# All transfers of the first batch ahead of the first weights, and products of a zero tile behind the first ten steps of a fused retention and mixer kernel

## The chip, the cores and the metric

The kernel runs on one core of a Trainium2 chip. The metric is the device time of one execution in microseconds (us), and less is better. The core has five engines that run side by side and wait for one another by semaphores: TensorE (PE in the rows; PEld is its weight load), VectorE (DVE), ScalarE (ACT), GpSimd (POOL) and SyncE (SP). SP issues every transfer of this kernel. The clock of TensorE has two levels, 1.2 and 2.4 GHz, and the rows show the granted share as PEclk, 0.50 or 1.00.

## What is computed

Three stages follow each other on 8 batches of 576 positions, 8 heads of 64 channels (512 channels in all):

```python
scores = q @ k.T / 8;  ret = scores * gamma[h] ** (i - j) for i >= j, else 0
x = ret @ v                                   # retention, heads side by side
u = x + (x.T @ U @ V).T                       # mix over positions, rank 32
x2 = u + relu(u @ w_ch1) @ w_ch2              # 512 -> 2048 -> 512
xk, xr = mu * x2 + (1 - mu) * x2_prev         # each position with the one before
out = sigmoid(xr @ w_r) * (relu(xk @ w_k) ** 2 @ w_v)
```

U, V and the weights arrive as float64 words and are turned into float32 on the chip.

## The kernel before

**Steps.** Retention is done in chunks of 64 positions: nine steps for each batch, 72 in all, listed in `seq` and run by `step_of(i)`. A step issues four groups of sixteen 64x64 products each: `scores(i+1)` (L792) for the next step, `inter(i)` (L817, the queries with the state), and `own(i)` (L833 the new state, L845 the chunk itself). VectorE then does `decay(i+1)` (L804) and, in `leave(i)`, three operations: y (L866), the state w (L878) and the output xt (L884). Tile `up` holds the scores and the inter products, `dn` the own products; each has one buffer. Every second step a finished block of 128 positions is transposed (`natural`, L892), copied by ScalarE as xs (L902), and some steps later multiplied with U (`low_rank`, L913). GpSimd scales each piece of k by a table (`scale_k`, L763).

**After a batch.** Step 10 starts with `low_rank_sum(0)`: ScalarE copies the sum (gs, L928) and casts it (gt, L932 and L935), and VectorE makes a remainder (L934). Eight products with V follow (`mix`, L943), VectorE adds them to xt (L947), `split_u` makes two parts of the result, and from then on `hidden(1)` issues twelve dense 128x512 products (L336) in each step: the product of u with w_ch1. These are the hidden products.

**Weights.** A weight piece (128x512 words, 512 KB) takes four stages, made by `convert`: load (a transfer to w_raw), down (ScalarE, L104, to `ca`, which has two buffers), fill (three VectorE operations, L110, L114 and L119) and split (ScalarE casts the first part, L127, and GpSimd subtracts to get the second, L128). `place(get, down, fill, split)` hangs the stages of the next weight piece in the list `waiting` on numbers of steps in `early`, and `stages(i)` issues those of step i behind the step's own work; numbers below zero stand for places ahead of step 0. So for the first four pieces (0, 4), (0, 5), (2, 6), (2, 8) say: loaded at step 0, 0, 2, 2 and filled at step 4, 5, 6, 8. U and V go the same way.

**Order.** The whole is under a manual schedule: each engine runs its instructions in the order of the code. SP's queue is one of these; its transfers use eight semaphores in turn, so a transfer is issued when the one eight places earlier has landed. `load_to(i)` issues the loads of q with k (qk) and k with v (kv), two chunks to a piece, that are due by step i. Twelve products of a zero tile (`warm`, L1039, 128x512) stand ahead of step 0.

Of the kernel before, what the change touches and what calls it, by code (L numbers as in the profile page):

```python
# [30 lines left out]
NL = S // L  # L31
KD = DM // 128
WARM = 12
# [6 lines left out]
def retention_mixer_kernel(ctx: ExitStack, tc: tile.TileContext, io):  # L40
    nc = tc.nc
# [22 lines left out]
    def bank(n, nm):  # L64
        return psum[-1].tile([128, 512], F32, tag=f"b{n}", name=nm, bufs=1)

    turns = {}


    def turn(kind, banks, nm):  # L70
        i = turns.get(kind, 0)
        turns[kind] = i + 1
        return bank(banks[i % len(banks)], nm)
# [58 lines left out]
    waiting, going = [], []  # L132
# [13 lines left out]
    class Weight:  # L146
# [45 lines left out]
        def load(self, pool, j):  # L192
            for lo, parts in enumerate((self.h, self.l)):
                parts[j] = unit(pool, F32R, f"{self.nm}u{j}{lo}")
                nc.sync.dma_start(parts[j].bitcast(F32), self.kept[:, 2 * j:2 * j + 2, lo])
# [536 lines left out]
    with ExitStack() as st:  # L732
# [27 lines left out]
        def scale_k(b, p):  # L760
            n = 2 if p < NC - 1 else 1
            k = kv[b, p][:, :n, :256].rearrange("p c (h d) -> p c h d", d=D)
            nc.gpsimd.tensor_tensor(k, k, ktab[:, p, :n].to_broadcast([128, n, NP, D]), op=ALU.mult)  # L763
# [271 lines left out]
        warm = ac.tile([128, 1, 128], BF16, name="warm")  # L1035
        nc.vector.memset(warm, 0.0)
        nc.scalar.copy(omu[:, 0, 0:1], warm[:, 0, 0:1])
        for i in range(WARM):
            nc.tensor.matmul(  # L1039
                turn("u", ("n", "g"), f"warm{i}"),  # L1040
                warm[:, 0, :],
                warm.to_broadcast([128, 4, 128]),
                start=True,
                stop=True,
            )


        early = {}

        def place(*steps):  # L1050
            for i, stage in zip(steps, [x for x in waiting.pop(0) if x]):
                early.setdefault(i, []).append(stage)

        def stages(i):
            for stage in early.pop(i, []):
                stage()

        prep_u()
        place(-3, 0, 1, 2)
        place(-3, 1, 2, 3)  # L1060
        prep_v()
        place(-2, 2, 3, 4, 5)
        for w in w1:
            w.convert(big, big)
        for n, (get, fill) in enumerate((
            (0, 4), (0, 5), (2, 6), (2, 8), (5, 9), (6, 10), (7, 11), (8, 12),
            (9, 13), (9, 13), (10, 14), (11, 15), (12, 16), (12, 16), (13, 17), (14, 18),
        )):
            place(get, fill - 1, fill, fill + 1)

        for w in wv:
# [8 lines left out]
        def load_to(i):  # L1080
            while units and units[0][0] <= i:
                load(*units.pop(0)[1:])
# [1 line left out]
        load_to(0)  # L1084
        nc.sync.dma_start(dtab, io["dtab"])
        nc.sync.dma_start(ktab, io["ktab"])
        stages(-3)
        load_to(2)
        nc.sync.dma_start(qtab[:, 0], io["qtab"])
        nc.sync.dma_start(step, io["step"])  # L1090
        stages(-2)
        nc.sync.dma_start(ident, io["ident"])
        scale_k(0, 0)
        scores(0)
        decay(0)
        load_to(5)

        def next_qtab(p):
            for a in range(NP):
# [8 lines left out]
        def plan(i, fn, *args, where=due):  # L1108
            where.setdefault(i, []).append((fn, args))

        def step_of(i):
            b, c = seq[i]
            load_to(i + (5 if i < 4 or i > 11 else 4))
            for fn, args in first.pop(i, []):
                fn(*args)
            if i + 1 < N:
                nb, ncx = seq[i + 1]
                if ncx % 2 == 0:
                    scale_k(nb, ncx // 2)
                scores(i + 1)  # L1120
            inter(i)
            if i + 1 < N:
                decay(i + 1)
            own(i)
            leave(i)
            if c % 2 == 1 or c == NL - 1:
                last = c == NL - 1
                wait = 4 if i < 6 else 2 if last or b < 2 else 3
                plan(i + 1, natural, b, c // 2)
                where = first if last and b == 0 else due  # L1130
                plan(i + wait, low_rank, b, c // 2, where=where)
                if last and b == 0:
                    plan(i + wait, low_rank_sum, b, where=first)
                    plan(i + wait, later, b)
                elif last:
                    plan(i + wait, low_rank_sum, b)
                    plan(i + wait + 1, later, b)
            if i < 2 * NC - 2 and i % 2 == 0:
                next_qtab(i // 2 + 1)
            for fn, args in due.pop(i, []):  # L1140
                fn(*args)
            if not ready:
                mixes(9)
            few = i < 2 * NL + 2 or c == 7 or c == 4 and b > 3
            hidden(1 if few else 2, False)
            stages(i)
            if b > 1 and i > 2 * NL + 3 and not todo:
                quiet.append(i)
                slot(new=len(quiet) % 2 == 1)

        for i in range(N):
            step_of(i)
# [216 lines left out]
    for q in range(NB // 2 + 1):  # L1369
# [5 lines left out]
        if not last:  # L1375
            gates(q, (mine, other), 1 if q else 2)
            PUMP[0] = 2
            for g in range(NG):
                n = q * NG + g
# [101 lines left out]
```

## Time and profile before

| what | value |
|---|---|
| three runs | 1369.38, 1372.71, 1373.61 us |
| their median | 1372.71 us |
| profiled execution: span from the first to the last instruction | 1371.8 us (no other time is listed for it) |
| TensorE busy in the span | 1345.0 us, 98% |
| VectorE, ScalarE, GpSimd busy | 922.3, 625.0, 367.0 us |
| moved by transfers | 307.63 MB, mean 224 GB/s |

Shares of busy time are means over stages of very different kinds. TensorE's pipelined products count as busy while they are under way, at either clock, so a busy TensorE can still run at half its pace; PEclk tells which. In a row of the timeline, the number in brackets is how long the engine sat idle before, and the arrow names what ended that.

### The profile page before, as it was taken

Reading aid. Unit: us, or ns where it says so; the run is one execution under the profiler, and the core shown is the slowest. Engines: PE = TensorE matmul, PEld = TensorE weight load, DVE = VectorE, ACT = ScalarE, POOL = GpSimd, SP = SyncE. Lnnn points to the kernel's source line nnn. Section 1 sums busy time; section 2 is a strip of 40 time slices with the busy share of each in tenths; the row PEclk is TensorE's granted clock in tenths of the full one; section 3 lists DMA queues with packets and bytes.
Section 4 is the critical chain, followed back from the end, with each engine's and each line's share of the span. In section 5 each row is a group of like instructions: output and inputs, shape, how many; then the busy total and the mean of one; then the engine's idle time right before and its main releaser. Section 6 shows DMA issues by size and latency. Waiting matters only on the chain.

```text
span 1371.8 us, 26093 instructions
## 1 busy us (share of the span) xinstructions
PE 1345.0 (98%) x10296; PEld 1098.9 (80%) x10296; DVE 922.3 (67%) x1347; ACT 625.0 (46%) x1089; POOL 367.0 (27%) x301
## 2 busy tenths in 40 slices
PE   6899999999999999999999999999999999999998
PEld 4677777777877878887888888888888888888897
DVE  5873445342334156999798898687787787787753
ACT  4443334343333445554444544565455465465431
POOL 3250232322221245222211232203303303304212
PEclk8799999999999999999999999999999999999999
DMA  9667586967746475969888796797085075174272
GB/s 343 234 219 235 184 295 230 304 210 277 242 163 213 165 238 209 344 207 315 274 278 279 239 323 222 245 309 270 0 291 200 25 282 184 41 275 145 100 281 80
DMA packets 122762, 307.63 MB, mean 224 GB/s; under 512 B 15120, under 2 KB 27792, under 8 KB 122640
## 3 DMA queue, kind: packets, MB, share of 16 engines
q1 hardware_dynamic: 122640, 305.96, 64.5%
q8 instruction: 81, 1.33, 0.4%
q14 instruction: 41, 0.34, 0.1%
HBM read 214.69 MB, written 91.23 MB: 223 GB/s over the span
## 4 chain that ended last, share of the span: by engine, by line
PE 62%; DVE 2%; issue 0%; DVEq 0%
PE v L1326 14%; PE gc L521 6%; PE ga L521 6%; PE gd L521 6%; PE h L336 5%; PE kd L1230 4%; PE kc L1230 4%; PE ka L1230 4%; PE gb L521 3%; PE kb L1230 2%; PE rd L1230 2%; PE rc L1230 2%; PE ra L1230 2%; PE c L602 1%; PE c L601 1%; PE c L603 1%
## 5 line engine op out<-in xcount | busy, mean ns | idle before, releaser
L342 ACT ACTIVATE hs<-h 128x512 f32<-128x512 f32 x144 | 85.8, 598 | 249.3 <-PE h L336 241.4
L804 DVE TENSOR_TENSOR pm<-up,dtab 128x256 f32<-128x256 f32 x72 | 30.4, 422 | 164.0 <-PE up L817 148.2
L1282 POOL TENSOR_TENSOR vl<-m,vh 128x512 fp32r<-128x512 f32 (+1 forms) x40 | 47.7, 1194 | 310.1 <-ACT vh L1281 238.8
L480 ACT CAST sbh<-rb 128x1024 fp32r<-128x1024 f32 x64 | 67.4, 1053 | 54.0 <-PE gd L521 41.2
L1326 PE MATMUL v<-vh,wv_0u 128*128 128x512 f32 x288 | 88.7, 389 | 0.0
L1326 PE MATMUL v<-vh,wv_1u 128*128 128x512 f32 x288 | 88.6, 389 | 0.0
L481 DVE TENSOR_TENSOR sbl<-rb,sbh 128x1024 fp32r<-128x1024 f32 x64 | 85.3, 1333 | 1.9 <-ACT sbh L480 1.7
L481 DVE TENSOR_TENSOR sal<-ra,sah 128x1024 fp32r<-128x1024 f32 (+1 forms) x64 | 65.4, 1022 | 18.8 <-PE gd L521 10.9
L480 ACT CAST sah<-ra 128x1024 fp32r<-128x1024 f32 (+1 forms) x64 | 53.6, 837 | 53.7 <-DVE ra L462 21.1
L1282 POOL TENSOR_TENSOR vl<-c,vh 128x512 fp32r<-128x512 f32 (+1 forms) x40 | 62.2, 1575 | 25.9 <-ACT vh L1281 25.9
L1326 PEld LDWEIGHTS v<-vh,wv_1u 128*128 128x128 f32 x288 | 54.1, 188 | 11.2
L1326 PEld LDWEIGHTS v<-vh,wv_0u 128*128 128x128 f32 x288 | 53.9, 188 | 11.1
L947 DVE TENSOR_TENSOR xt<-mx,xt 128x256 f32<-128x256 f32 x64 | 28.8, 458 | 50.1 <-PE mx L943 50.1
L1281 ACT CAST vh<-m 128x512 fp32r<-128x512 f32 (+1 forms) x40 | 23.2, 579 | 75.3 <-DVE m L1280 75.3
L1326 PE MATMUL v<-vl,wv_0u 128*128 128x512 f32 x144 | 56.0, 389 | 0.0
L1326 PE MATMUL v<-vl,wv_1u 128*128 128x512 f32 x144 | 56.0, 389 | 0.0
L565 POOL TENSOR_TENSOR x<-x,ur 128x512 f32<-128x512 f32 x16 | 24.5, 1546 | 107.7 <-DVE x L561 51.2
L634 ACT ACTIVATE tp<-x2l,omu 128x511 f32<-128x511 f32 x72 | 50.9, 713 | 2.5 <-DMA x2l<-xb 2.5
L763 POOL TENSOR_TENSOR kv<-kv,ktab 128x512 f32<-128x512 f32 (+1 forms) x40 | 40.5, 1017 | 42.7 <-DMA kv<-in_kv 36.3
L792 PEld LDWEIGHTS up<-qk 64*64 64x64 f32 x1152 | 24.4, 137 | 31.8 <-issue 28.2
L538 POOL TENSOR_TENSOR m<-m,ur 128x512 f32<-128x512 f32 x8 | 12.3, 1554 | 126.3 <-ACT m L535 126.3
L1280 DVE SCALAR_TENSOR_TENSOR m<-m 128x512 f32<-128x512 f32 (+1 forms) x40 | 44.8, 1120 | 1.4
(289 smaller groups left out, 3876.4 us busy)
## 6 DMA issues: line engine op xcount, KB each, us to landing
wk<-keys SPq DMA_DIRECT2D x80, 512.0 KB, 6.0
hp<-hs SPq DMA_DIRECT2D x128, 256.0 KB, 3.4
rb<-hp SPq DMA_DIRECT2D x64, 512.0 KB, 6.1
wr<-gates SPq DMA_DIRECT2D x40, 512.0 KB, 7.1
qk<-in_qk SPq DMA_DIRECT2D x32, 512.0 KB, 5.0
kv<-in_kv SPq DMA_DIRECT2D x32, 512.0 KB, 5.6
ra<-hp SPq DMA_DIRECT2D x32, 512.0 KB, 6.9
ur<-ub SPq DMA_DIRECT2D x18, 512.0 KB, 5.9
```

What stands on the lines that cost most here:

```text
L336: nc.tensor.matmul(hps[t, f], w.part(lo, k, fo), u[k // 2][:, k % 2, :], start=(part == 0 and k == 0), stop=(part == 2 and k == KD - 1),)
L342: nc.scalar.activation(h, hps.pop((t, f)), AF.Relu)
L480: nc.scalar.copy(hi_, src)
L481: nc.vector.tensor_tensor(lo_, src, hi_.bitcast(F32), op=ALU.subtract)
L521: nc.tensor.matmul(group[g][p], l[:, col(p)], r, start=(h == 0 and j == 0 and i == 0), stop=(i == 2 and last), skip_group_check=True,)
L634: nc.scalar.activation(tp[:, 1:], x[:, :BT - 1], AF.Copy, scale=omu[:, j, k:k + 1])
L763: nc.gpsimd.tensor_tensor(k, k, ktab[:, p, :n].to_broadcast([128, n, NP, D]), op=ALU.mult)
L804: nc.vector.tensor_tensor(m, t[:, :, 0:128].rearrange("p g (a i) -> p g a i", i=L), dtab, op=ALU.mult)
L1230: nc.tensor.matmul(ps[b], l, r[:, i], start=(part == 0 and i == 0 and j == 0), stop=(i == 1 and j == 2), skip_group_check=True,)
L1280: nc.vector.scalar_tensor_tensor(x, x, 0.0, x, op0=ALU.max, op1=ALU.mult)
L1282: eng.tensor_tensor(l, x, h.bitcast(F32), op=ALU.subtract)
L1326: nc.tensor.matmul(vacc[t][o], w.part(lo, g, col(o)), x[:, i, :], start=(g == 0 and i == 0 and j == 0), stop=(g == NG - 1 and i == 1 and j ...
```

## The change

`idle(n, banks)` issues n products of the zero tile into the named banks of PSUM. It takes the place of the loop ahead of step 0, stands with three products behind the stages of each of the steps 0 to 9, and with four ahead of the scores that step 10 issues. The loads of all of batch 0's q, k and v are moved ahead of those of the first weights (`load_to(5)`, `load_to(6)`, `load_to(8)` ahead of step 0), and U and V behind some of them. U and V are converted two steps later. The first four weight pieces are all loaded at step 0 and filled at steps 7, 8, 8 and 8; the table of the later pieces is as it was.

```diff
@@ -1035,15 +1035,17 @@
         warm = ac.tile([128, 1, 128], BF16, name="warm")
         nc.vector.memset(warm, 0.0)
         nc.scalar.copy(omu[:, 0, 0:1], warm[:, 0, 0:1])
-        for i in range(WARM):
-            nc.tensor.matmul(
-                turn("u", ("n", "g"), f"warm{i}"),
-                warm[:, 0, :],
-                warm.to_broadcast([128, 4, 128]),
-                start=True,
-                stop=True,
-            )
-
+        def idle(n, banks):
+            for _ in range(n):
+                nc.tensor.matmul(
+                    turn("u", banks, f"warm{turns.get('u', 0)}"),
+                    warm[:, 0, :],
+                    warm.to_broadcast([128, 4, 128]),
+                    start=True,
+                    stop=True,
+                )
+
+        idle(WARM, ("n", "g"))
 
         early = {}
 
@@ -1056,16 +1058,23 @@
                 stage()
 
         prep_u()
-        place(-3, 0, 1, 2)
-        place(-3, 1, 2, 3)
+        place(-3, 2, 3, 3)
+        place(-3, 3, 4, 4)
         prep_v()
-        place(-2, 2, 3, 4, 5)
+        place(-2, 4, 5, 6, 7)
         for w in w1:
             w.convert(big, big)
-        for n, (get, fill) in enumerate((
-            (0, 4), (0, 5), (2, 6), (2, 8), (5, 9), (6, 10), (7, 11), (8, 12),
+        lead = [[x for x in waiting.pop(0) if x] for _ in range(4)]
+        for n, stage, i in (
+            (0, 0, 0), (1, 0, 0), (2, 0, 0), (3, 0, 0),
+            (0, 1, 6), (0, 2, 7), (1, 1, 7), (0, 3, 8), (1, 2, 8), (2, 1, 8), (1, 3, 8),
+            (2, 2, 8), (3, 1, 8), (2, 3, 8), (3, 2, 8), (3, 3, 9),
+        ):
+            early.setdefault(i, []).append(lead[n][stage])
+        for get, fill in (
+            (5, 9), (6, 10), (7, 11), (8, 12),
             (9, 13), (9, 13), (10, 14), (11, 15), (12, 16), (12, 16), (13, 17), (14, 18),
-        )):
+        ):
             place(get, fill - 1, fill, fill + 1)
 
         for w in wv:
@@ -1084,16 +1093,18 @@
         load_to(0)
         nc.sync.dma_start(dtab, io["dtab"])
         nc.sync.dma_start(ktab, io["ktab"])
-        stages(-3)
         load_to(2)
         nc.sync.dma_start(qtab[:, 0], io["qtab"])
         nc.sync.dma_start(step, io["step"])
-        stages(-2)
+        load_to(5)
         nc.sync.dma_start(ident, io["ident"])
+        stages(-3)
         scale_k(0, 0)
         scores(0)
         decay(0)
-        load_to(5)
+        load_to(6)
+        stages(-2)
+        load_to(8)
 
         def next_qtab(p):
             for a in range(NP):
@@ -1113,6 +1124,8 @@
             load_to(i + (5 if i < 4 or i > 11 else 4))
             for fn, args in first.pop(i, []):
                 fn(*args)
+            if i == NL + 1:
+                idle(4, (0, 1))
             if i + 1 < N:
                 nb, ncx = seq[i + 1]
                 if ncx % 2 == 0:
@@ -1144,6 +1157,8 @@
             few = i < 2 * NL + 2 or c == 7 or c == 4 and b > 3
             hidden(1 if few else 2, False)
             stages(i)
+            if i <= NL:
+                idle(3, (0, 1))
             if b > 1 and i > 2 * NL + 3 and not todo:
                 quiet.append(i)
                 slot(new=len(quiet) % 2 == 1)
```

On SP's queue, from batch 0's piece 2 on (qk_0 and kv_0 behind w_0 are batch 1's), before:

```order
L754 DMA qk_2_187<-in_qk 128x1024
L756 DMA kv_2_189<-in_kv 128x1024
L160 DMA w_0_raw_229<-in_moe_w_ch 128x512
L160 DMA w_0_raw_231<-in_moe_w_ch 128x512
L754 DMA qk_3_233<-in_qk 128x1024
L756 DMA kv_3_235<-in_kv 128x1024
L160 DMA w_0_raw_343<-in_moe_w_ch 128x512
L160 DMA w_0_raw_345<-in_moe_w_ch 128x512
L754 DMA qk_4_347<-in_qk 128x512
L756 DMA kv_4_349<-in_kv 128x512
L754 DMA qk_0_461<-in_qk 128x1024
L756 DMA kv_0_463<-in_kv 128x1024
```

and now:

```order
L754 DMA qk_3_186<-in_qk 128x1024
L756 DMA kv_3_188<-in_kv 128x1024
L1011 DMA vraw<-in_moe_V 32x144 x4
L754 DMA qk_4_195<-in_qk 128x512
L756 DMA kv_4_197<-in_kv 128x512
L160 DMA w_0_raw_235<-in_moe_w_ch 128x512
L160 DMA w_0_raw_237<-in_moe_w_ch 128x512
L160 DMA w_0_raw_239<-in_moe_w_ch 128x512
L160 DMA w_0_raw_241<-in_moe_w_ch 128x512
L754 DMA qk_0_475<-in_qk 128x1024
L756 DMA kv_0_477<-in_kv 128x1024
```

The pieces 3 and 4 of batch 0 stood behind two and four weight pieces; now all four weight pieces stand behind them. Piece 2 has moved up too, ahead of U and V (`uraw`, `vraw`).

On VectorE, at the end of batch 0 (names with numbers: pm8, y7, xt0 are step 8's decay and step 7's results in batch 0; w1_0_raw2 is the third of the first four weight pieces), before:

```order
L119 SCALAR_TENSOR_TENSOR cf_590<-w1_0_raw2_343,cf_590 128x512
L804 TENSOR_TENSOR pm8_618<-up8_601,dtab_114 128x256
L866 TENSOR_TENSOR y7_637<-up8_601,qtab_115 128x256
L878 TENSOR_TENSOR w0_7_639<-dn7_620,w0_6_572 128x256
L884 TENSOR_TENSOR xt0_219<-dn7_620,y7_637 128x4x64
L804 TENSOR_TENSOR pm9_670<-up9_653,dtab_114 128x256
L866 TENSOR_TENSOR y8_681<-up9_653,qtab_115 128x256
L884 TENSOR_TENSOR xt0_219<-dn8_672,y8_681 128x4x64
L110 TENSOR_SCALAR cf_691<-ca_648 128x512
L114 SCALAR_TENSOR_TENSOR cf_691<-ca_648,cf_691 128x512
L119 SCALAR_TENSOR_TENSOR cf_691<-w1_0_raw3_345,cf_691 128x512
```

and now:

```order
L866 TENSOR_TENSOR y8_709<-up9_681,qtab_115 128x256
L884 TENSOR_TENSOR xt0_227<-dn8_700,y8_709 128x4x64
L110 TENSOR_SCALAR cf_721<-ca_670 128x512
L114 SCALAR_TENSOR_TENSOR cf_721<-ca_670,cf_721 128x512
L119 SCALAR_TENSOR_TENSOR cf_721<-w1_0_raw1_237,cf_721 128x512
L110 TENSOR_SCALAR cf_731<-ca_725 128x512
L114 SCALAR_TENSOR_TENSOR cf_731<-ca_725,cf_731 128x512
L119 SCALAR_TENSOR_TENSOR cf_731<-w1_0_raw2_239,cf_731 128x512
L110 TENSOR_SCALAR cf_739<-ca_735 128x512
L114 SCALAR_TENSOR_TENSOR cf_739<-ca_735,cf_739 128x512
L119 SCALAR_TENSOR_TENSOR cf_739<-w1_0_raw3_241,cf_739 128x512
```

A fill used to have the operations of a step on either side; now three fills stand in a row behind step 8's xt0, ahead of the decay of step 10.

On TensorE, from step 1's own products to step 2's first group (up3 are the scores of step 3), before:

```order
L833 MATMUL dn1_257<-kv0_0_156 64x64 x8
L845 MATMUL dn1_257<-pm1_200,kv0_0_156 64x64 x8
L792 MATMUL up3_285<-qk0_1_163 64x64 x8
L817 MATMUL up3_285<-qk0_1_163,w0_1_276 64x64 x8
L833 MATMUL dn2_304<-kv0_1_165 64x64 x8
```

and now:

```order
L833 MATMUL dn1_269<-kv0_0_156 64x64 x8
L845 MATMUL dn1_269<-pm1_208,kv0_0_156 64x64 x8
L1040 LDWEIGHTS warm_123
L1040 MATMUL warm15_291<-warm_123 128x512
L1040 MATMUL warm16_293<-warm_123 128x512
L1040 MATMUL warm17_295<-warm_123 128x512
L792 MATMUL up3_297<-qk0_1_160 64x64 x8
L817 MATMUL up3_297<-qk0_1_160,w0_1_288 64x64 x8
```

The products of the zero tile stand between a step's own products and the next step's scores; the weight load stands ahead of each of the three.

## Rows read from the trace of the kernel before

**Rows 1.** The page: the span; one group (busy us, mean ns of one).

```profile
span 1371.8 us, 26093 instructions
...
L804 DVE TENSOR_TENSOR pm<-up,dtab 128x256 f32<-128x256 f32 x72 | 30.4, 422 | 164.0 <-PE up L817 148.2
```

**Rows 2.** Windows: length; busy us (count) by engine; PEclk, DMA share, GB/s.

```profile
0.00:10.00 10.00, 7.55 (x140) 3.98 (x140) 1.34 (x4) 2.12 (x4) 1.46 (x6) 1.00 0.85 281
...
10.00:20.00 10.00, 5.19 (x205) 4.25 (x200) 7.23 (x25) 5.44 (x18) 1.88 (x2) 1.00 0.94 310
...
20.00:29.00 9.00, 5.54 (x152) 4.58 (x156) 6.56 (x16) 6.08 (x18) 4.63 (x6) 0.80 1.03 409
...
29.00:39.00 10.00, 8.63 (x191) 6.53 (x184) 8.99 (x17) 3.90 (x8) 4.56 (x4) 0.50 1.03 407
...
39.00:42.40 3.40, 1.99 (x73) 1.37 (x72) 0.00 (x0) 3.15 (x8) 2.04 (x2) 1.00 0.24 95
...
42.40:47.90 5.50, 3.23 (x9) 2.20 (x9) 5.36 (x14) 1.87 (x4) 0.23 (x1) 0.50 0.00 0
...
47.90:52.60 4.70, 4.70 (x11) 3.41 (x12) 4.29 (x7) 1.31 (x3) 0.00 (x0) 0.50 0.74 250
...
52.70:95.00 42.30, 42.30 (x785) 33.10 (x785) 35.69 (x66) 23.50 (x46) 22.71 (x18) 1.00 0.79 275
...
95.00:1371.80 1276.80, 1265.73 (x8751) 1039.34 (x8749) 852.80 (x1202) 577.61 (x985) 329.51 (x265) 1.00 0.64 220
```

**Rows 3.** TensorE's timeline, 14 to 58 us: start, us, engine, line, operation, count.

```profile
14.48 0.46 PE L792 MATMUL up<-qk 64*64 64x64 f32 x16 [1.20 <-DMA qk<-in_qk]
...
16.14 0.46 PE L792 MATMUL up<-qk 64*64 64x64 f32 x16 [0.50 <-DVE y L866]
...
21.23 0.70 PE L792 MATMUL up<-qk 64*64 64x64 f32 x15 [3.04 <-DVE cf L110]
...
28.68 0.67 PE L792 MATMUL up<-qk 64*64 64x64 f32 x16
...
30.56 0.65 PE L913 MATMUL gall<-xs,ust 128*32 128x128 f32 x8
...
47.88 2.21 PE L336 MATMUL h<-uh,w_0h 128*128 128x512 f32 x4 [0.68 <-DVE xt L947]
...
53.11 0.46 PE L792 MATMUL up<-qk 64*64 64x64 f32 x16
...
54.20 0.66 PE L892 MATMUL xn<-ident,xt 128*128 128x128 f32 x4
...
54.61 1.18 PE L336 MATMUL h<-uh,w_0h 128*128 128x512 f32 x4
...
57.54 0.46 PE L792 MATMUL up<-qk 64*64 64x64 f32 x16
```

**Rows 4.** The chain that ended last, one piece: start, us, what, count.

```profile
487.37 73.75 PE h L336 x324
```

**Rows 5.** The timeline of all engines around one fill.

```profile
28.89 0.42 DVE L110 TENSOR_SCALAR cf<-ca 128x512 uint32<-128x512 uint32 x1
...
29.27 0.62 ACT L127 CAST w_0h<-cf 128x512 fp32r<-128x512 f32 x1
...
29.34 0.69 DVE L114 SCALAR_TENSOR_TENSOR cf<-ca,cf 128x512 uint32<-128x512 uint32 x1
...
29.97 1.27 POOL L128 TENSOR_TENSOR w_0l<-cf,w_0h 128x512 fp32r<-128x512 f32 x1 [2.64 <-ACT w_0h L127]
...
30.06 1.72 DVE L119 SCALAR_TENSOR_TENSOR cf<-w_raw,cf 128x512 uint32<-128x512 uint32 x1
```

**Rows 6.** The timeline ahead of the mixing.

```profile
40.19 0.69 ACT L104 ACTIVATE ca<-w_raw 128x512 f32<-128x512 f32 x1
...
40.78 1.05 ACT L928 COPY gs<-gall 32x128 f32<-32x128 f32 x4
...
42.51 0.68 DVE L934 TENSOR_TENSOR gt<-gs,gt 32x512 fp32r<-32x512 f32 x1 [3.52 <-ACT gt L932]
```

## Prediction

> **What bounds the kernel now.** I read the span on the page first [rows 1], then a table of stages [rows 2]: what matters there is TensorE's busy share, the granted clock and the transfer rate. From 95 us to the end TensorE is busy 1265.73 of 1276.80 us, and from 52.7 to 95 us all of the time, at the full clock. So the end follows the moment at which the dense hidden products begin; what is gained ahead of it comes off the total, unless it is given back later. That moment is the row at 47.88 in TensorE's timeline [rows 3]. Ahead of it lies a head in which TensorE works in small pieces: 5.19 of 10 us busy from 10 to 20, 5.54 of 9 from 20 to 29, and then 8.63 of 10 at half clock from 29 to 39. Two waits stand out: 1.20 us for a piece of batch 0's qk (14.48) and 3.04 us ahead of the row at 21.23, a step that reads the next piece (the profile names a conversion on VectorE there, which these products don't read). The transfers run at 409 and 407 GB/s in 20 to 39, their ceiling here, but only at 310 GB/s in 10 to 20, where the small rows of U and V fill places in SP's queue. The head ends on a chain: ScalarE copies the low-rank sum (40.78), VectorE waits 3.52 us for it (42.51) [rows 6], the mixing products follow, and the first hidden product comes 5.37 us after 42.51, at half clock: its twelve products take 53.11 - 47.88 = 5.23 us, the next twelve 57.54 - 54.61 = 2.93 [rows 3].
>
> **The change, part by part.**
>
> *Transfers.* Batch 0's q, k and v are 2 x 4.5 x 0.524 = 4.72 MB by their shapes; the tables, U and V with them make 5.49 MB. The first 10 us move 2.81 MB [rows 2]; the rest at 409 GB/s takes 6.6 us, so all has been moved at 16.6 us. Landing comes later. Now, the piece awaited at 21.23 has 5.50 MB issued up to it, and these had been moved at 18.7 us (2.81 MB, then 310 GB/s): at most 2.5 us of lag. So batch 0 is there between 16.6 and 19.1 us, and its last piece is first used in step 7, after 22. The wait of 1.20 goes, and that of 3.04. The first weights (four of 0.524 MB) land by 21.7 to 24.2, batch 1's first qk by 23.0 to 25.5. What is late next is the small identity table: it now stands behind two pieces of 0.524 MB, and the transpose of step 2 needs it at about 12.
>
> *Pace of the steps.* At full clock the four groups of a step's small products take 54.20 - 53.11 = 1.09 us and a transpose 0.41 more; at half clock the four groups take 30.56 - 28.68 = 1.88 [rows 3]. Three added products cost 3 x 73.75/324 = 0.68 us at full clock [rows 4]. They stand behind a step's own products and ahead of the next scores, where TensorE would wait for VectorE's y (0.50 us at 16.14); so 0.18 to 0.68 us a step shows, and I charge all of it. Step 3's scores without their wait start at 14.48 - 1.20 = 13.3. The added products of steps 0 to 2 and the identity push this to at most 13.3 + 3 x 0.68 = 15.3; I take 13.9, since TensorE is half idle there [rows 2]. Step 3 then takes 1.77, and steps 4 to 7, each with a transpose or a low-rank product (charged as a transpose), 2.18. Step 7 begins at 13.9 + 1.77 + 3 x 2.18 = 22.2, and its VectorE work, behind 1.09 us of products, is over about 0.8 us later, at 24.1.
>
> *Conversion of the first weights.* All four pieces are now filled at steps 7 (one) and 8 (three). A fill is 0.42 + 0.69 + 0.69 = 1.80 us of VectorE [rows 5], and there is a new neighbour. A filled piece is cast by ScalarE (0.62), and then GpSimd subtracts (1.27), while VectorE is in the next fill. The group [rows 5] shows what happens then: GpSimd starts at 29.97, and the VectorE operation of 30.06 takes 1.72 us instead of 0.69, until 0.54 us past GpSimd's end. Before, only one fill of the first weights met this, because the others had steps between them. The Trainium skill (SBUF — State Buffer, Who interferes with whom) makes it a lock that the first of the two holds for a whole instruction, so that up to 1.27 us are lost at each meeting; the row has 1.03. By the rule the three would cost 0.7 us more, and 1369.5 would come out of the sum below.
> Fill 0 ends at 24.1 + 1.8 = 25.9. Step 8's three VectorE operations (0.42 each [rows 1], less what they overlap, 1.0 in all) give 26.9. Three fills with a meeting each, 3 x 2.83 = 8.5, end at 35.4; without one, 3 x 1.80, at 32.3. This is the dear part of the change: the same 7.2 us were spread over steps 4 to 8 before, partly in VectorE's idle time.
>
> *From the last fill to the hidden products.* Two queues run in parallel. ScalarE casts (0.62), prepares another weight (0.69), copies the sum (1.05) and casts it (0.6, from 40.78 + 1.05 to 42.51): 38.4. VectorE does step 10's decay (0.4) and a fill with its meeting (2.83): 38.6. The later one starts what stood at 42.51, so that this comes 3.9 us earlier, and the hidden products at 44.0 instead of 47.88. The four products ahead of step 11's scores (0.91 us at full, 1.75 at half clock) lie in the wait for the low-rank sum and cost nothing; uncovered they would cost at most 1.75.
>
> *The clock at that point.* TensorE again has nothing to do between step 9's last product, near 30, and the low-rank product, near 35. Between 42.4 and 47.9 it was busy 3.23 of 5.50 us and the clock stayed at 0.50 [rows 2]; the same mixing products stand there now. I take the first twelve hidden products at half clock as before. Zero difference, with 2.3 us (5.23 - 2.93) to win.
>
> *Given back later?* All transfers up to the last ones ahead of the mixing land before 42.4 (95 GB/s in 39 to 42.4, none after [rows 2]); the 1.0 MB that 10 to 20 us fall short of 409 GB/s return 2.4 us, so that they land before 40 and still ahead of 44. Weights to come are filled in the same order against the hidden products, and TensorE waits for none of them in 52.7 to 95. I charge nothing; the bound is VectorE's slack there, 42.30 - 35.69 = 6.6 us.
>
> The sum: 1371.8 - 3.9 = 1367.9 for the span. The median of the three runs shown, 1372.71, is 0.9 above this span, so 1368.8.
>
> **The rivals.**
> - *As summed*, 1368.8, between 1367.2 (the steps hide 0.3 us of the added products each) and 1370.2 (step 3 at 15.3).
> - *The clock holds.* If the added products have it at full when the hidden ones begin, 2.3 us more are won: 1366.5. For it: the four products, the scores and step 10's work form some 4 us without a pause just ahead of the mixing. Against it: 42.4 to 47.9 [rows 2], where the mixing did not raise the clock. The Trainium skill (TensorE: Matmul & The Clock Gate, HAM oscillation) says that an engine left idle begins its next burst at half rate, and the added products work against that; the head agrees, and no run here shows the products doing it.
> - *VectorE and GpSimd don't meet.* Fills end at 32.3. ScalarE then decides: behind the third cast, over at 31.1, stand a preparation (0.69), three copies of step 9 (1.3, two casts' worth by size), and then the four operations (3.0), to 36.1. That is 6.4 us earlier than 42.51: 1366.3. Against it: the casts follow each fill at once, so GpSimd starts inside the next one, as at 29.97.
> - *The head hardly moves.* Step 3 only at 15.3, and 0.3 us more in each of steps 3 to 7, since VectorE's y and xt come late as at 16.14: 2.9 us of the gain go, 1371.7.
> - *Slower: the clock falls early and the added products become the pace.* At half clock a step takes 1.88 + 3 x 0.44 (5.23/12) = 3.19 instead of 1.77, with 0.41 more for its transpose. From step 3 on, 5 x 1.42 + 4 x 0.41 = 8.7 us are lost, 4.8 more than is won: 1377.5. It decides only if the clock is down by step 4, at about 16 us; in steps 6 and 7 alone it costs 3.7 and eats up the gain. Against it: 10 to 20 us kept the full clock with TensorE half idle [rows 2].
>
> **How the numbers follow.** Chances: as summed 0.45, the clock holds 0.20, no meeting 0.14, hardly moves 0.15, slower 0.06. About 0.3%, 4.1 us, is what a measurement of this kernel can tell from no change. The sum's 3.9 lies on that bound, so its chance is split, 0.19 faster and 0.26 within; with the next two, faster gets 0.53, within 0.42 (with the fourth and a little of the last), slower 0.05. The range goes from clock and meeting both being favourable, 1364, to a little above the head that hardly moves, 1372.2; 1364.5 leaves out the corner.
>
> **What would show it.** Right: no wait for qk or kv behind step 2; the last piece used at about 24; step 8's three fills as a block of some 8.5 us on VectorE with single operations of 1.6 to 1.8 us; TensorE idle some 4 to 5 us ahead of the low-rank product; the first hidden product near 44. Wrong: a granted clock of 0.50 between 10 and 25 us; fills of 1.8 us throughout; a first twelve that take 3 us; TensorE waits for weights between 50 and 95 us.

## The result, and the profile after

| what | before | after |
|---|---|---|
| median, us | 1373.16 (1369.38 to 1374.30, 4 runs) | 1380.99 (1378.40 to 1382.34, 4 runs) |
| span of the profiled execution, us | 1371.8 | 1378.2 |
| first hidden product (L336), us | 47.88 | 55.40 |
| scores behind the first twelve, us | 53.11 | 60.09 |

The ratio is 1.0058 with a 95% interval of 1.0043 to 1.0074: the change made the kernel slower, where 1368.8 us and a gain were forecast. The median lies 8.8 us above the upper end of the range. Line numbers of after: the products of the zero tile are L1040, the other lines of the head are as before.

The windows of after answer to [rows 2]; the last shows that the dense part hasn't changed (the one before it still holds some of the late head):

```profile
10.00:20.00 10.00, 7.23 (x226) 4.82 (x215) 6.47 (x21) 4.64 (x15) 3.04 (x4) 1.00 0.99 330
20.00:29.00 9.00, 5.16 (x146) 3.54 (x147) 3.61 (x12) 1.99 (x6) 0.60 (x1) 0.96 0.98 363
29.00:39.00 10.00, 7.92 (x189) 5.11 (x192) 6.29 (x15) 5.88 (x15) 2.54 (x6) 0.86 1.03 412
...
42.40:47.90 5.50, 2.17 (x12) 0.63 (x12) 5.36 (x8) 3.84 (x10) 2.94 (x3) 0.77 0.00 1
...
52.70:95.00 42.30, 41.62 (x644) 32.06 (x645) 38.76 (x71) 21.14 (x39) 18.26 (x14) 0.93 0.78 266
95.00:1378.20 1283.20, 1272.73 (x8907) 1044.97 (x8905) 857.73 (x1211) 582.71 (x995) 333.99 (x268) 1.00 0.63 220
```

In 95 us to the end TensorE is idle 10.5 us, and was idle 11.1 before. So the 6.4 us of the span were lost in the head. There, from 20 to 29 us, TensorE is busy 5.16 and VectorE 3.61 of 9.00 us (5.54 and 6.56 in [rows 2]): neither holds up the other by its work. TensorE's timeline of after, against [rows 3]:

```profile
13.52 0.66 PE L892 MATMUL xn<-ident,xt 128*128 128x128 f32 x4 [1.11 <-DMA ident<-in_ident]
...
14.75 0.33 PE L792 MATMUL up<-qk 64*64 64x64 f32 x4
15.48 0.39 PE L792 MATMUL up<-qk 64*64 64x64 f32 x11 [0.40 <-issue]
...
20.32 0.55 PE L892 MATMUL xn<-ident,xt 128*128 128x128 f32 x3 [1.59 <-issue]
...
28.09 0.27 PE L833 MATMUL dn<-kv 64*64 64x64 f32 x1 [3.52 <-issue]
...
29.67 1.49 PE L1040 MATMUL warm<-warm 128*128 128x512 bf16 x3
31.09 0.71 PE L792 MATMUL up<-qk 64*64 64x64 f32 x16
...
36.31 0.34 PE L817 MATMUL up<-qk,w 64*64 64x64 f32 x5 [2.08 <-issue]
...
45.73 0.65 PE L913 MATMUL gall<-xs,ust 64*32 64x128 f32 x8 [4.96 <-ACT xs L902]
...
55.40 2.21 PE L336 MATMUL h<-uh,w_0h 128*128 128x512 f32 x4 [0.68 <-DVE xt L947]
...
60.09 0.46 PE L792 MATMUL up<-qk 64*64 64x64 f32 x16
```

No step waits for qk or kv any more. In the place of those waits stand four stalls put down to "issue", that is, to nothing that the profile shows: 0.40 + 1.59 + 3.52 + 2.08 = 7.6 us. All four begin in the middle of a group of products (the second behind 1 of 4 transposes, the third behind 14 of 16 own products), at instructions for which the trace records no semaphore to wait for. The same thing had one long row before, and it was not among those that the prediction read:

```profile
27.83 0.34 PE L845 MATMUL dn<-pm,kv 64*64 64x64 f32 x5 [2.23 <-issue]
```

A short one, 0.17 us, stands at 41.27 in before. The 1.34 us put down to "issue" at 32.55 in before are another thing: they stand ahead of a whole group of scores, which begins 0.1 us behind the end of VectorE's y.

**Where the stalls stand.** Windows from the span's start to within a stall give the number of matmuls and of weight loads that TensorE has done by then (first and second count). Of after, to the second, third and fourth stall:

```profile
0.00:19.50 19.50, 14.80 (x349) 8.65 (x349) 7.11 (x22) 6.76 (x19) 4.38 (x8) 1.00 0.90 305
0.00:27.00 27.00, 19.06 (x476) 11.41 (x476) 11.08 (x34) 8.75 (x25) 4.99 (x9) 1.00 0.92 315
0.00:35.50 35.50, 25.20 (x603) 15.31 (x603) 15.31 (x44) 13.16 (x37) 7.24 (x14) 0.95 0.94 338
```

From stall to stall it is exactly 127 matmuls and 127 loads, 254 instructions. The trace also records TensorE's semaphore instructions, which the windows leave out. With them the four stalls of after stand behind 449, 705, 961 and 1217 instructions, 256 apart, and the row at 27.83 of before stands behind 961 as well. The stalls belong to places in TensorE's instruction stream, not to any work. The page of after has a queue for such a thing:

```profile
PE 1349.6 (98%) x10330; PEld 1098.6 (80%) x10330; DVE 927.4 (67%) x1347; ACT 625.4 (45%) x1089; POOL 367.1 (27%) x301
...
q8 instruction: 81, 1.33, 0.4%
```

81 packets in 1.33 MB are 16.4 KB each, and TensorE's 20660 instructions are 80.7 times 256 (81.5 times with the semaphore instructions and a few more that the page doesn't count). So each packet brings TensorE a block of 256 instructions. The packets' times, read from the trace of each kernel (us; "entered" is the first instruction of the block before):

| kernel | entered | fetch of the next block | stalled until |
|---|---|---|---|
| before | 14.65 | 18.73 to 19.73 | no stall (idle for qk until 21.23) |
| before | 21.55 | 25.41 to 26.51 | 27.83 |
| after | 15.48 | 17.87 to 18.98 | 20.32 |
| after | 20.32 | 25.69 to 26.65 | 28.09 |
| after | 28.09 | 33.86 to 34.89 | 36.31 |

In each row that stalls TensorE goes on 1.3 to 1.4 us behind the fetch's end, and the fetch begins 2.4 to 5.8 us after TensorE has entered the block before. So a block takes at least those plus 1.0 and 1.4: 4.8 to 8.2 us here, however fast its products are. In the table's first row the fetch fell into the wait of 3.04 us for qk [rows 3] and cost nothing. The change took that cover away.

### The profile page after: what moved, and what is told of

Its sections match the earlier page's. It is cut to its first block, busy times and chain, and to the rows that moved or that the text cites. A ratio compares the mean times of both kernels' runs of the same rounds, so it can differ in the third digit from the quotient of the medians.

```text
span 1378.2 us, 26149 instructions
## 1 busy us (share of the span) xinstructions
PE 1349.6 (98%) x10330; PEld 1098.6 (80%) x10330; DVE 927.4 (67%) x1347; ACT 625.4 (45%) x1089; POOL 367.1 (27%) x301
## 3 DMA queue, kind: packets, MB, share of 16 engines
q8 instruction: 81, 1.33, 0.4%
## 4 chain that ended last, share of the span: by engine, by line
PE 61%; DVE 2%; issue 1%; DVEq 0%
PE v L1341 14%; PE ga L521 6%; PE gc L521 6%; PE gd L521 6%; PE h L336 5%; PE kd L1245 4%; PE kc L1245 4%; PE ka L1245 4%; PE gb L521 3%; PE kb L1245 2%; PE rd L1245 2%; PE rc L1245 2%; PE ra L1245 2%; PE c L603 1%; PE c L601 1%; PE c L602 1%
## 5 line engine op out<-in xcount | busy, mean ns | idle before, releaser
L1341 PEld LDWEIGHTS v<-vh,wv_0u 128*128 128x128 f32 x288 | 53.9, 188 | 11.1
```

The costliest lines, as they stand in the source:

```text
L1341: nc.tensor.matmul(vacc[t][o], w.part(lo, g, col(o)), x[:, i, :], start=(g == 0 and i == 0 and j == 0), stop=(g == NG - 1 and i == 1 and j ...
```

## The experiments

Two theories stand against each other. The theory of the fetch (F): the head's pace is that of TensorE's instruction blocks, whose fetch comes late when many data transfers are in flight. The theory of the pace (P): the head is long by its own work, that is, the added products, the half clock, and the late fills that GpSimd holds up. Each has parts that can be taken away alone. In the table, "stalls" are those put down to "issue" at the block ends, in order; times before on the same chips were 1371.9 to 1372.4.

| run | median, us | ratio, 95% interval | first hidden | stalls, us |
|---|---|---|---|---|
| e1 | 1377.45 | 1.0041 (1.0025 to 1.0057) | 52.53 | 0.91, 3.51, 0.51 |
| e2 | 1374.66 | 1.0014 (1.0004 to 1.0025) | 51.70 | 4.07, 0.96, 0.79 |
| e3 | 1376.50 | 1.0034 (1.0019 to 1.0049) | 52.78 | 0.94, 2.41, 1.88, 0.42 |
| e4 | 1375.86 | 1.0027 (1.0016 to 1.0038) | 51.48 | 1.60, 0.23 |
| e5 | 1371.02 | 0.9995 (0.9983 to 1.0007) | 45.33 | 1.89 |
| e6 | 1372.74 | 1.0009 (0.9998 to 1.0020) | 48.97 | 1.23, 3.70 |
| e7 | 1372.84 | 1.0002 (0.9993 to 1.0012) | 49.22 | 2.34, 1.05 |
| e8 | 1375.51 | 1.0021 (1.0009 to 1.0034) | 49.59 | 1.43, 0.53, 3.78 |
| e9 | 1380.01 | 1.0058 (1.0040 to 1.0076) | 55.23 | 1.86, 0.23, 2.48 |
| e10 | 1378.21 | 1.0042 (1.0028 to 1.0056) | 52.74 | 2.13, 1.76, 3.06 |
| e11 | 1372.83 | 1.0001 (0.9989 to 1.0013) | 48.45 | 1.10, 2.71, 0.39 |
| e12 | 1374.05 | 1.0013 (1.0002 to 1.0023) | 50.08 | 1.98, 1.48, 1.66 |

In every run each stall listed stands behind 449, 705, 961 or 1217 instructions (the last of e11 behind 1473), whatever the order of transfers. First hidden product and stalls are read from one execution each. The executions of one kernel lie between 0.8 us (e10) and 6.9 us (e6) apart, so differences of 1 or 2 us between two traces are not told from chance.

### The change without the products, and the products alone (e1, e2)

e1 is after with

```diff
-            if i == NL + 1:
-                idle(4, (0, 1))
...
-            if i <= NL:
-                idle(3, (0, 1))
```

and e2 is before with these four lines and `idle`.

> The changed kernel without the 30 + 4 added products of the zero tile; the new order of transfers and conversions stays. Theory F (fetch): TensorE's stalls with no visible cause stand at fixed counts of its instructions (after the 449th, 705th, 961st and 1217th, 256 apart), because its next instructions come by a transfer that queues behind the data; without the products TensorE only comes to each count earlier and waits longer there. So the stalls stay, at the same counts, and 1 to 4 us of 1381 are won: 1377 to 1380. Theory P (the products themselves are the pace): 10 steps by 0.74 us, 7 us and more are won: 1371 to 1374.

> The kernel before with nothing but the 34 products of the zero tile added. Theory F: 68 more instructions ahead of the hidden products move TensorE's stalls to earlier steps and the products fill part of the waits; 1 to 4 us slower than before, 1374 to 1377, with stalls at the same counts of instructions. Theory P: 6 to 8 us slower, 1379 to 1381, the whole loss of the change. Should the clock stay full up to the hidden products and the products hide in the waits, 1371.

The products account for 2.9 of the 7.5 us by which the first hidden product of after is late (52.53 against 55.40), and for 1.7 thousandths of the ratio, some 2.3 us, though the two intervals overlap. The rest stays without them, with a stall of 3.51 us. Alone they make before slower, though its transfers haven't moved, and its stalls have grown. Both times are where F had them, and outside P's. e2's timeline and windows:

```profile
21.71 0.55 PE L892 MATMUL xn<-ident,xt 128*128 128x128 f32 x3 [4.07 <-issue]
```

```profile
0.00:19.00 19.00, 15.04 (x349) 8.71 (x349) 8.48 (x28) 6.26 (x18) 3.33 (x7) 1.00 0.89 288
...
0.00:28.50 28.50, 21.10 (x476) 12.54 (x476) 13.76 (x38) 13.54 (x38) 7.69 (x13) 0.94 0.94 328
```

The counts, 349 and 476, are those of after, at other times and under another order of transfers. A step now has six instructions more, so the ends of blocks come earlier in the program. In before the second of them stood just behind the start of the scores that wait for qk (the row at 21.23 of [rows 3]); here it stands ahead of them, the fetch runs from 19.41 to 20.32, and that wait for qk is gone, inside the stall of 4.07.

What the products were meant for, they did in the head. PEclk from 10 to 45 us is 0.85 in e2 and 0.77 in before, and in after and e1:

```profile
10.00:45.00 35.00, 22.08 (x579) 14.42 (x568) 22.20 (x53) 15.43 (x42) 9.62 (x12) 0.95 0.87 321
```

```profile
10.00:45.00 35.00, 21.77 (x588) 17.20 (x592) 25.85 (x56) 17.59 (x48) 11.17 (x13) 0.74 0.86 317
```

Alone, in e2, the clock that they held up did not pay for their instructions and the longer stalls.

### The change with its fills spread (e3)

```diff
-            (0, 1, 6), (0, 2, 7), (1, 1, 7), (0, 3, 8), (1, 2, 8), (2, 1, 8), (1, 3, 8),
-            (2, 2, 8), (3, 1, 8), (2, 3, 8), (3, 2, 8), (3, 3, 9),
+            (0, 1, 4), (0, 2, 5), (1, 1, 5), (0, 3, 6), (1, 2, 6), (2, 1, 6), (1, 3, 7),
+            (2, 2, 7), (3, 1, 7), (2, 3, 8), (3, 2, 8), (3, 3, 9),
```

> The changed kernel with the first weights filled at steps 5, 6, 7 and 8 instead of 7, 8, 8 and 8 (prepared a step ahead, cast a step behind). Both theories: two to three of the fills of 2.7 us move from the block behind step 8 into waits of VectorE, and the hidden products begin 4 to 6 us earlier: 1375 to 1377. If the block of fills is not what the hidden products wait for, no change: 1380 to 1382.

The time is as expected, but the first hidden product comes only 2.6 us earlier instead of 4 to 6, with stalls of 5.7 instead of 7.6 us. Both changed, so this run alone doesn't say which of them gave the time.

### Two transfers in flight (e4, e5)

SyncE's queue gets, ahead of each load behind batch 0's pieces, a transfer of one word that reads the tile of the load two places earlier, for the first sixteen loads. e4 is after with it, e5 is before with it.

```diff
+    def paced(x):
+        if len(flying) < 16:
+            flying.append(x)
+            n = len(flying) - 1 - 2
+            if n >= 0:
+                nc.sync.dma_start(pace[n:n + 1, :], flying[n])
```

> The changed kernel, but from the first weights on a load is issued only when the load two before it has landed (a transfer of one word, that reads the landed tile, holds SP's queue); two instead of eight are in flight. Theory F: the instructions no longer queue behind megabytes of data; the stalls after the 961st and 1217th instruction, 3.5 and 2.1 us, shrink below 1 us each and the clock does not fall at 28 us: 4 to 7 us faster than the changed kernel, 1374 to 1377. Theory P, or any theory of the products, the fills or the clock alone: no gain, 1380 to 1383, and slower still if the weights now come late.

> The kernel before with the rule of two loads in flight from the first weights on, and nothing else of the change. Theory F: its stalls after the 961st instruction (2.2 us) and at 32.5 us shrink below 1 us each and the clock holds longer; 2 to 4 us faster than before, 1368 to 1370, unless batch 0's pieces, which now also wait behind the rule, come later. Without theory F: no gain or a loss, 1372 to 1376, since transfers only get slower.

e4's windows and its stalls:

```profile
20.00:25.00 5.00, 4.77 (x148) 3.20 (x147) 3.08 (x11) 1.99 (x6) 0.00 (x0) 1.00 0.71 219
25.00:30.00 5.00, 3.22 (x82) 1.78 (x80) 4.04 (x10) 4.41 (x12) 1.20 (x4) 1.00 0.71 220
```

```profile
19.74 0.55 PE L907 MATMUL xn<-ident,xt 128*128 128x128 f32 x3 [1.60 <-issue]
...
24.23 0.27 PE L848 MATMUL dn<-kv 64*64 64x64 f32 x1 [0.23 <-issue]
```

In e4 the rate is 219 GB/s from 20 to 25 and 220 from 25 to 30 us, and of the stalls 1.8 of 7.6 us are left. The time is where F had it, and the interval of its ratio lies wholly below that of the change. The fetch begins 2.1 and 3.3 us after TensorE has entered a block (21.85 for 19.74, 27.51 for 24.22) instead of 5.4 and 5.8. 3.9 us are won at the first hidden product; what came in their place is a wait of 2.52 us for batch 1's qk, now late, and the fills with their meetings. In e5 the stall at 27.72 stays, 1.89 us, where less than 1 was expected: batch 0's own pieces are not limited, and the rate is 352 GB/s from 14 to 20 and 317 from 20 to 25. The next block is fetched 1.2 us after its entry, no later one is waited for, and the first hidden product comes 2.5 us earlier than before. The ratio doesn't tell that from no change.

### Everything together, with and without the products and the limit (e6, e7, e8)

All three spread the fills as in e3 and load the identity ahead of piece 1. e6 has no products and a limit of three, e7 the products and the limit, e8 neither.

```diff
         nc.sync.dma_start(ktab, io["ktab"])
+        nc.sync.dma_start(ident, io["ident"])
         load_to(2)
```

> The changed kernel with four edits: fills of the first weights at steps 5, 6, 7 and 8, the identity table ahead of the second piece of q and k, three loads in flight from the first weights on, and none of the 34 added products. Theory F: stalls at 961 and 1217 below 1 us, one fill behind step 8, hidden products near 40 to 44 instead of 55.4; 1364 to 1369, faster than the kernel before by 4 to 8 us. If something else than fetches and fills bounds the head, 1372 or more.

> As e6, but with the 34 products of the zero tile. Theory F: with fetches quick and the fills spread, the products cost at most 0.7 us in each step that TensorE paces and move the fixed counts by a quarter of a block: 1 to 5 us slower than e6, 1367 to 1372. If they hold the clock up to the first hidden products, these take 2.9 instead of 5.2 us and it comes out level with e6.

> As e6, but with eight loads in flight, as the kernels before and after have it. Theory F: the stall after the 961st instruction is back with 2 to 4 us; 2 to 5 us slower than e6. Without theory F: as e6, or faster, because the data come sooner.

None beats before, so that what F forecast for e6 was missed by 3.7 us and more. With the limit (e6, e7) they equal it; without it (e8) the ratio is 1.0021. The products neither cost nor win anything there: e6 and e7 have the same time, though the first twelve hidden products of e7 still took 5.46 us, and not 2.9. A stall of 3.70 us is left in e6, its fetch 4.4 us behind the entry at 309 GB/s: the limit of three doesn't settle it. e8 has the same stall, 3.78 us, without the limit, and the intervals of e6 and e8 overlap, so this pair says nothing of what the limit is worth. And a new wait is seen; e6's engines around it (L807 are the scores):

```profile
28.11 1.28 POOL L128 TENSOR_TENSOR w_0l<-cf,w_0h 128x512 fp32r<-128x512 f32 x1 [9.35 <-ACT w_0h L127]
28.23 1.70 DVE L114 SCALAR_TENSOR_TENSOR cf<-ca,cf 128x512 uint32<-128x512 uint32 x1
...
30.47 1.68 POOL L1034 CAST vst<-vl 32x144 fp32r<-32x144 f32 x4
```

```profile
31.72 0.71 PE L807 MATMUL up<-qk 64*64 64x64 f32 x16 [2.85 <-DVE y L881]
```

A fill that GpSimd holds up (1.70 instead of 0.69) delays VectorE's y behind it, and with it TensorE's next scores. In e8, e11 and e12 the same wait of 2.5 to 2.7 us is put down to "issue", but it stands ahead of a whole group of sixteen, and y ends 0.1 us ahead of it: it's this one, as it is the 1.34 us at 32.55 in before, and not counted in the table.

### No transfers while two blocks are fetched (e9)

```diff
+            if i == 7:
+                nc.sync.dma_start(held, pm[7][0:1, 0, 0, 0:1])
-            load_to(i + (5 if i < 4 or i > 11 else 4))
+            load_to(8 if i in (5, 6) else i + (5 if i < 4 or i > 11 else 4))
```

with the loads of the first weights moved from step 0 to step 7, and their later stages to 8 and 9; the loads of the next two pieces move to step 7 too.

> The change, but with nothing in flight while TensorE is in its blocks 705 to 961 and the end of the one before: SyncE's queue waits, behind the last piece of batch 0, for the decay of step 7, and only then issues batch 1's first pieces and the first weights (prepared and filled at steps 8 and 9). If the stalls without a visible cause are instruction fetches held up by the transfers in flight, the stall at count 961 shrinks from 3.52 us to at most 0.7, the one at 705 from 1.59 to at most 1.0, and the stall at 1217, where everything is in flight again, stays at 1 us or more. If the fetch comes late whatever else is moved, 961 keeps 2.5 us or more. The time is no test here, since the weights arrive 5 us later: 1378 to 1386.

Windows of e9, and its stalls:

```profile
18.00:20.00 2.00, 0.38 (x11) 0.14 (x1) 1.83 (x8) 0.00 (x0) 1.20 (x2) 1.00 0.06 23
20.00:22.00 2.00, 1.76 (x46) 1.20 (x50) 0.00 (x0) 1.17 (x4) 0.46 (x1) 1.00 0.00 0
22.00:24.00 2.00, 2.00 (x76) 1.19 (x71) 1.83 (x6) 0.81 (x3) 0.00 (x0) 1.00 0.03 8
24.00:26.00 2.00, 1.77 (x58) 1.43 (x49) 1.71 (x6) 0.09 (x1) 0.00 (x0) 1.00 0.00 0
26.00:28.00 2.00, 2.00 (x76) 1.31 (x75) 1.19 (x5) 1.93 (x6) 0.73 (x3) 1.00 0.88 233
...
30.00:32.00 2.00, 0.00 (x0) 0.00 (x0) 0.00 (x0) 0.00 (x0) 1.04 (x1) 1.00 0.99 389
```

```profile
20.24 0.55 PE L892 MATMUL xn<-ident,xt 128*128 128x128 f32 x3 [1.86 <-issue]
...
24.73 0.27 PE L833 MATMUL dn<-kv 64*64 64x64 f32 x1 [0.23 <-issue]
...
32.38 0.37 PE L817 MATMUL up<-qk,w 64*64 64x64 f32 x3 [2.48 <-issue]
```

With 0 GB/s in the window of the entry (20.24), the fetch begins after 2.05 us (22.29) and the stall is 0.23 us: in after, the same block's took 5.37 and 3.52. The next block is entered at 24.73 and the transfers are back from 26.1 us on, sooner than the 2.05 us that a fetch took with nothing in flight; this fetch begins only after 5.24 us (29.97), and the stall is 2.48. TensorE's instructions up to there and the clock (1.00) are the same; the transfers differ. That is the run that decides for F. The other kernels with the products bear it out at the same place, behind 705 instructions: the fetch begins 2.1 us after the entry in e4, with 215 GB/s in between, 3.0 in e7 (321 GB/s), and 4.6 to 5.4 in after, e2, e3 and e10 (346 to 406 GB/s). The first stall stayed at 1.86 where at most 1.0 was expected: its block was entered at 15.13, with batch 0's last pieces still on the way. The time, 1380.01, is that of after, since the weights come later: ahead of the last low-rank product TensorE now waits 7.29 us instead of 4.96.

### The casts behind all fills (e10)

```diff
-            (0, 1, 6), (0, 2, 7), (1, 1, 7), (0, 3, 8), (1, 2, 8), (2, 1, 8), (1, 3, 8),
-            (2, 2, 8), (3, 1, 8), (2, 3, 8), (3, 2, 8), (3, 3, 9),
+            (0, 1, 6), (0, 2, 7), (1, 1, 7), (1, 2, 8), (2, 1, 8),
+            (2, 2, 8), (3, 1, 8), (3, 2, 8), (0, 3, 9), (1, 3, 9), (2, 3, 9), (3, 3, 9),
```

> The change, but the casts and GpSimd's subtractions of the first three pieces stand at step 9, behind all fills. If the meeting of VectorE and GpSimd costs what the trace shows (1.64 instead of 0.69 us for an operation), the three fills in a row take 5.4 to 6.2 us instead of 8.3, the first hidden product comes some 2 us earlier (53.3), and the time is 1378.5 to 1379.5 against 1381. If TensorE's own pace (instruction stalls, half clock, added products) sets the head's end and not the fills, the first hidden product stays within 0.7 us of 55.4 and the time at 1380 to 1382.

First after, where GpSimd subtracts (L128) while VectorE fills, then e10, where it doesn't:

```profile
37.90 0.42 DVE L110 TENSOR_SCALAR cf<-ca 128x512 uint32<-128x512 uint32 x1
...
38.71 1.47 POOL L128 TENSOR_TENSOR w_0l<-cf,w_0h 128x512 fp32r<-128x512 f32 x1 [5.07 <-ACT w_0h L127]
39.07 1.65 DVE L119 SCALAR_TENSOR_TENSOR cf<-w_raw,cf 128x512 uint32<-128x512 uint32 x1
...
44.55 1.64 DVE L119 SCALAR_TENSOR_TENSOR cf<-w_raw,cf 128x512 uint32<-128x512 uint32 x1
...
48.68 1.49 POOL L763 TENSOR_TENSOR kv<-kv,ktab 128x512 f32<-128x512 f32 x1
...
49.29 1.41 DVE L934 TENSOR_TENSOR gt<-gs,gt 32x512 fp32r<-32x512 f32 x1
```

```profile
36.91 0.42 DVE L110 TENSOR_SCALAR cf<-ca 128x512 uint32<-128x512 uint32 x1
...
38.09 0.69 DVE L119 SCALAR_TENSOR_TENSOR cf<-w_raw,cf 128x512 uint32<-128x512 uint32 x1
...
41.66 0.69 DVE L119 SCALAR_TENSOR_TENSOR cf<-w_raw,cf 128x512 uint32<-128x512 uint32 x1
```

Three fills take 44.55 + 1.64 - 37.90 = 8.3 us in after and 41.66 + 0.69 - 36.91 = 5.4 in e10, as expected of the meetings. They also began 1.0 us earlier, and of the 3.8 us by which they end earlier 1.2 were lost again: the first hidden product comes 2.7 us earlier. So a part of P holds too: behind the stalls, these fills are on the path. In the time it is less clear, as the intervals of the two ratios overlap.

### Piece 2 of batch 0 alone (e12), and with two in flight (e11)

Before, with piece 2 and the identity ahead of U and V, and U and V converted as in the change; e11 has the limit of e5 as well.

```diff
-        stages(-3)
         load_to(2)
...
-        stages(-2)
         nc.sync.dma_start(ident, io["ident"])
+        load_to(5)
+        stages(-3)
...
-        load_to(5)
+        stages(-2)
```

> The kernel before with piece 2 of batch 0 and the identity ahead of U and V (their conversion as in the change), and at most two loads in flight from the first weights on; no added products, first fills where they were before. If the transfers in flight are what holds up the instruction fetches: no wait for qk at 21, all stalls without a visible cause together under 3 us, first hidden product at 43 to 45.5, time 1369 to 1370.5. If the stalls come whatever is in flight, the gain at 21 is lost at the next block: 46.5 to 48, 1371.5 to 1373.

> The same without the limit: all eight transfers in flight. If the gain of an earlier piece 2 is eaten by instruction stalls, the stall at count 961 (2.23 us before) grows to 3 us or more, or one of 1 us or more comes at 705, and the first hidden product is not before 46.5: 1371.5 to 1374. If the wait for the piece is what the head loses, as the prediction had it, the first hidden product comes at 44.5 to 45.5 and the time is 1369 to 1370.

e12's waits and stalls:

```profile
15.29 0.27 PE L792 MATMUL up<-qk 64*64 64x64 f32 x2 [1.98 <-issue]
...
20.66 0.48 PE L792 MATMUL up<-qk 64*64 64x64 f32 x5 [0.89 <-DMA qk<-in_qk]
22.62 0.58 PE L792 MATMUL up<-qk 64*64 64x64 f32 x10 [1.48 <-issue]
...
28.73 0.48 PE L845 MATMUL dn<-pm,kv 64*64 64x64 f32 x5 [1.66 <-issue]
```

In e12 the 1.20 us for qk are gone and the 3.04 have become 0.89, and the stalls have grown from 2.4 to 5.1 us, with new ones behind 449 and 705 instructions: most of what was won goes into the instruction blocks, and the time, 1374.05, is no gain. The first hidden product comes even 2.2 us later than before. The wait for y has its part in that (2.53 us against 1.34), and the clock: from 18 to 40 us PEclk is 0.50, and 0.69 in before. e11 missed: 4.2 us of stalls instead of less than 3, and a wait of 2.54 us for piece 3 that I hadn't seen coming, since two weights stand ahead of that piece.

## Why the prediction was wrong

**The step that failed is "Pace of the steps".** It charged a step by its products, at 1.77 and 2.18 us, and let step 7 begin at 22.2. It began at 31.09. The first hidden product came at 55.40 against 44.0, and the 11.4 us between them are these:

- The start of step 3: 14.75 against 13.9, +0.8. The identity was late as written (1.11 us).
- Steps 3 to 6: 16.34 us against 8.31, +8.0. Of that 5.51 are the first three stalls. Step 6, 3.52 aside, took 1.7 more than charged, most of it at the half clock that followed the longest stall: the granted clock was down from 28.3 to 31.7 us, the three products took 1.49 us there, and 0.82 elsewhere.
- From step 7 to the fills: 6.8 us against 4.7, +2.1, the fourth stall.
- The three fills with GpSimd: 8.3 against 8.5; from there to gt 3.1 against 3.2. Both right. On the meetings the Trainium skill (SBUF — State Buffer, Who interferes with whom) has a lock held for a whole instruction; the trace agrees in kind, with L119 at 1.64 instead of 0.69 and ending 0.5 us behind GpSimd. The loss was 0.95 a meeting, and 1.03 in [rows 5].
- From gt to the hidden products: 6.1 against 5.4, +0.7. gt itself met GpSimd's scaling of batch 1's k and took 1.41 instead of 0.68 [rows 6].

**What the step left out was in the traces.** 16.34 us hold some two blocks, and a block needs its fetch's delay, 1.0 and 1.4 us. In before, the wait for qk hid one such fetch, and the row at 27.83 showed the next. I took the wait of 3.04 for a loss to be won back. By the table, the next block could not have begun before 19.73 + 1.4 = 21.1 us (an estimate, with the fetch as it was), and TensorE entered it at 21.55: hardly 0.4 us of the 3.04 were there to be won. e12 shows that 2.15 of it went, and 2.7 of stalls came.

**Transfers.** Right: no wait for batch 0. But that they were denser was charged nothing. 363 instead of 409 GB/s from 20 to 29 us is no denser than before [rows 2]; 330 instead of 310 in 10 to 20 is. What e9 shows is that with transfers in flight at all, a fetch begins up to 3.3 us later.

**The clock.** Half at the first twelve hidden products, as charged (4.69 us against 5.23), again behind an idle stretch (4.96 us ahead of 45.73). The rival in which the clock holds was wrong: the products mostly held it up to 45 us, as e1 beside after shows, but not across that stretch. What the Trainium skill (TensorE: Matmul & The Clock Gate, HAM oscillation) says of an idle engine's next burst agrees with 45.73, and the four products there ran at half clock themselves (1.89 us).

**The rival on the slow side** gave 1377.5, nearest to the result, for another reason: the clock did not fall by 16 us. Its number is no merit of its mechanism.

**Given back later.** Right: [rows 2] and the last window of after differ by no more than 0.6 us of idle time. Of the 7.5 us by which the first hidden product was late, the end was late by 6.4; the first twelve, 0.5 us shorter, and these 0.6 make up the difference.

**What stays open.** In the head the delay of a fetch behind the entry is 2.05 us with nothing in flight (e9), 0.5 to 3.3 in e4 at 83 to 215 GB/s, and 2.9 to 5.8 at 400 GB/s and above in all kernels here; but in e6 it is 4.4 at 309 GB/s, and in e11 3.9 at 344 and 4.7 at 226. Behind 1473 instructions, ahead of the mixing, it is 7.57 us in before (41.27 to 48.84) with no transfer in between, and 0.8 or less in eight of the other kernels, with none or next to none. So the rate alone doesn't give it, and transfers are not all that delays a fetch; when TensorE asks for a block, the profile doesn't show. Whether the number of transfers in flight, their place or their sizes decide was not tried apart. How the loss of 6.4 us splits between products, fills and transfers can't be told by sums either: taken away alone they give 2.9 (e1), 2.6 (e3), 2.7 (e10) and 3.9 us (e4) at the first hidden product, 12.1 in all, against 7.5 that were lost.

## What to carry to other kernels

Where an engine runs many short instructions beside dense transfers, count its instructions: a stall with no cause in the middle of a group, and again 256 instructions on, was the instruction stream here, and earlier data only moved the loss. Before a wait is taken away, look at what else it hides; here the fetch of a block lay in it. Each product that only keeps an engine busy is also two instructions to be fetched, its weight load and itself.

## What the runs showed of the hardware that was not expected

TensorE's instructions arrive in blocks of 256 (16.4 KB, 81 packets for 20660 instructions), while the program runs; the page counts these packets among those of the core's 16 DMA engines. In the head a fetch takes about 1.0 us and begins only after the block before has been entered; TensorE goes on 1.3 to 1.4 us behind its end in before and after. In the dense part (95 us to the end of after) 8907 + 8905 instructions take 1283.20 us, 18.4 us for 256, so that a delay of 6 us doesn't show; in the head a block is done in 4.2 us (20.32 to 24.57 in after, where the stall begins), and it does.
